# Top-k attention with a mixture-of-depths block: half a mask moved to VectorE, and the order of the last batch's end

## The chip, the cores and the metric

The kernel runs on one core of a Trainium2 chip. Its time is the device time of one execution in microseconds (us); the median of five runs counts. The core has five engines that run side by side and each work through their own instructions in order: PE (matrix products, with PEld for the loads of its stationary side), DVE (VectorE), ACT (ScalarE), POOL (GpSimd) and SP, which only issues transfers. They wait for each other by semaphores. PSUM is the memory that PE writes; it has eight banks, SBUF is the main memory on the chip.

## The reference

```python
# q, k, v: (8 batches, 8 heads, 576 rows, 64)
scores = scale * np.matmul(q, k.transpose(0, 1, 3, 2))
kth = np.partition(scores, -32, axis=-1)[..., -32:-31]
scores = np.where(scores >= kth, scores, -1000000000.0)
attn = np.exp(scores - max) ; attn = attn / (sum + 1e-09)
x = (attn @ v), heads side by side: (8, 576, 512)
# mixture of depths, for each batch b
s = einsum('bsd,d->bs', x, w_gate)
top_idx = the 128 rows with the largest s[b]
xe = x[b, top_idx]
h = np.maximum(xe @ w1, 0.0)          # 512 -> 1024
ye = h @ w2                           # 1024 -> 512
out[b] = x[b];  out[b, top_idx] += sigmoid(s[b, top_idx]) * ye
```

For each row of scores only the 32 largest count. Then, in each batch, the 128 rows of 576 with the largest gate go through a small network, whose result is added to these rows.

## The kernel before, in words

**Units and steps.** Each batch is cut into 18 units (`per_batch`): four row tiles of 128 with four pairs of heads each, and a last tile of 64 rows with two groups. There are 144 units. The main loop (`for n in range(-1, N)`) is a hand-written pipeline: step n works on several units at once, and the order of the calls is the order of the instructions on every engine (the wrapper `InOrder`, whose line 43 therefore stands for nearly all instructions in the profile). In step n the order is:

1. unit n-4: PE turns the scores and adds the mask to them (`weigh`, tile `ptr`), ACT takes exponentials (`pT`, `last`);
2. unit n-3: the mask `less`, scores below the 32nd largest (`mask_of`, `mask`): the first of two heads by ACT, the second by POOL, unless another pair of engines is passed as `on`;
3. unit n+1: PE multiplies q and k, ACT copies the scores out (`keep`, `sc<-ps`);
4. unit n-4: PE multiplies by v, ACT copies the sums out (`xs`);
5. unit n: DVE looks for a bound of the 32nd largest (`find_bound`: `cand`, `best`), then what has been put off for DVE (`flush_vector`), then what has been put off for POOL (`flush_pool`);
6. unit n-2: DVE finds the 32nd largest (`kth_of`: two MAX8 `next<-y`);
7. unit n-1: ACT marks what lies above the bound (`sides`), POOL multiplies scores by it (`y`, two operations and a small `y<-steps,seen`).

When a tile is done, DVE divides, POOL scales it into `x`, and two steps later DVE forms its gate (`prod<-x,wg`).

**The mixture** of a batch is a generator (`mixture`), advanced at fixed steps of the next two batches (`mix_at`, `mix_at_of`): spread the gates, count ranks, choose (`junk`, `pick`), gather 128 rows from the output by an indirect DMA on POOL (`fetch_rows`, `xe`), turn them (`xe_ps`, `xeT`), h in eight products of 128 columns (`multiply_h`), y in eight parts, and add to the output by an indirect DMA on POOL (`add_rows`, the scatter). For batches 0 to 4 the scatter is put off to POOL in the last step of the list, and issued in step 18b+55, that is, where n % 18 is 1.

**The end.** After the loop the last four units are finished by hand. The mixture of batch 6 (`between`) still has its eight parts of y to do. The mixture of batch 7 is the generator `closing`: the gate row is spread by PE transposes, DVE counts ranks and makes five `pick` tiles, PE multiplies them by places (`multiply_places`, tile `av`), DVE makes the row numbers (`keep_rows`), POOL gathers, PE turns the rows, and h, y and the scatter follow. Three parts of y of batch 6 stand ahead of its third stage, four ahead of the last counts and places, and the eighth behind the gather.

Between the gather and the turning of its rows stands a check: DVE folds some statistics of the whole run into one number per partition (`sure`), PE adds the partitions up (`av<-ones,sure`), DVE writes a flag (`unsure`), and `nc.values_load` loads the flag into a register of every engine. At the very end a branch on it would repeat everything by a general path, which this input doesn't need.

`xe_ps` and `y_ps` share the one buffer of the pool `ps_misc` (tag `misc`). `h` of the last batch lies in a tile `ptr` of two banks; `room_for_scores()` gives a tile of four.

```python
    def mask(sc, next8, on=None):
        less = wkpool.tile([P, 2, S], BF16, name="less")
        for i, engine in enumerate(on or (act, pool)):
```

## Time and profile before

| what | us |
|---|---|
| median of 5 runs | 878.7 |
| the five runs | 877.94, 878.58, 878.70, 881.25, 885.52 |
| the profiled execution | 881.17 |
| its span, first to last instruction | 879.31 |
| last score copy of ACT | 814.25 |
| last gather issued, landed | 846.26, 849.74 |
| last scatter issued, landed | 872.82, 877.75 |

The profile is one execution. Every time below is from the start of its span. Names such as `xe_ps<-ident,xe` say which tile is written from which. In a timeline a row may merge several instructions (x10); its length then runs from the first start to the last end. The time in brackets is how long the engine had stood still before the row, and what ended that. The durations of the indirect DMAs are those of their issue by POOL; the landing comes later.

### The profile page before, as it was taken

The numbers are of one execution on the slowest core, as the hardware profiler recorded it, in microseconds if no ns is written. First come the engines' busy times: TensorE is split into PE (matmuls) and PEld (weight loads), VectorE is DVE, ScalarE is ACT, GpSimd is POOL, SyncE is SP. The second block draws the span as 40 slices with busy tenths as digits, with TensorE's granted clock in tenths as the row PEclk, the third lists the DMA queues.
The fourth block names the chain that finished last, engine by engine and source line by source line (L and its number), as shares of the span: only waits on it lengthen the run. The fifth ranks groups of instructions, "written<-read, shape, count | busy, mean of one in ns | idle before, by whom it ended". The sixth has DMA issues, their size and how long they took to land. (4 is left out here: it accounts for less than half of the span.)

```text
span 879.3 us, 28118 instructions
## 1 busy us (share of the span) xinstructions
PE 808.7 (92%) x9879; PEld 620.6 (71%) x9879; DVE 810.9 (92%) x4918; ACT 760.5 (86%) x1705; POOL 708.2 (81%) x657
## 2 busy tenths in 40 slices
PE   4599988988999999999999999999999999988875
PEld 3377666666787777877787777877787778767743
DVE  4499999999999999999999999999999999999750
ACT  2599999988999999998999999999999999877710
POOL 2389998888888899888988899888988899878610
PEclk9599999999999999999999999999999999999988
DMA  5671111511141121511232122411333002101021
GB/s 120 162 211 26 38 26 55 105 38 38 61 83 43 38 50 56 105 38 38 74 72 54 38 41 65 105 38 27 86 52 73 14 15 68 15 14 14 13 68 15
DMA packets 122196, 50.36 MB, mean 57 GB/s; under 512 B 116416, under 2 KB 116416, under 8 KB 121024
## 3 DMA queue, kind: packets, MB, share of 16 engines
q1 hardware_dynamic: 118672, 43.91, 20.6%
q0 software_dynamic: 1792, 4.20, 2.8%
q8 instruction: 79, 1.29, 0.6%
q14 instruction: 69, 0.57, 0.2%
q10 hardware_dynamic: 1584, 0.39, 0.2%
HBM read 36.93 MB, written 11.55 MB: 55 GB/s over the span
## 5 line engine op out<-in xcount | busy, mean ns | idle before, releaser
L43 POOL TENSOR_TENSOR y<-sc,sides 128x576 f32<-128x576 f32 x288 | 370.5, 1324 | 107.4 <-ACT sides L43 104.8
L43 DVE MAX8 cand<-sc 128x8 f32<-128x72 f32 x2304 | 330.4, 218 | 21.0 <-ACT sc L43 21.0
L43 POOL TENSOR_SCALAR less<-sc,next 128x576 bf16<-128x576 f32 x141 | 248.9, 1765 | 17.6 <-DVE next L43 15.2
L43 PE MATMUL ptr<-out_of_reach,less 128*128 128x128 bf16 x1136 | 205.1, 220 | 22.3 <-POOL less L43 20.6
L43 ACT ACTIVATE sides<-sc,seen 128x576 bf16<-128x576 f32 x288 | 221.1, 768 | 4.8
L43 PE MATMUL ptr<-ident,sc 128*128 128x128 f32 x1136 | 215.7, 279 | 0.0
L43 DVE MAX8 next<-y 128x8 f32<-128x584 f32 x288 | 204.5, 752 | 3.6 <-POOL y L43 3.5
L43 PE MATMUL ps<-kT,qT 64*128 64x288 f32 (+1 forms) x1280 | 183.5, 435 | 5.4 <-ACT qT L43 3.5
L43 PEld LDWEIGHTS ptr<-ident,sc 128*128 128x128 f32 x1136 | 160.5, 141 | 22.4 <-PE av L43 10.4
L43 PE MATMUL av<-v,pT 128*64 128x65 f32 x4544 | 164.5, 225 | 11.5 <-ACT last L43 9.6
L43 PEld LDWEIGHTS av<-v,pT 128*64 128x64 f32 x4544 | 144.8, 138 | 41.4 <-ACT last L43 30.1
L43 ACT COPY sc<-ps 128x1152 f32<-128x1152 f32 x144 | 160.5, 1114 | 9.6 <-PE ps L43 9.3
L43 PEld LDWEIGHTS <-less 128*128 128x128 bf16 x1296 | 132.7, 103 | 44.3 <-POOL less L43 26.5
L43 ACT ACTIVATE pT<-ptr 128x1024 f32<-128x1024 f32 x142 | 143.9, 1013 | 17.8 <-PE ptr L43 15.5
L43 DVE MAX8 best<-cand 128x8 f32<-128x24 f32 (+2 forms) x864 | 141.9, 200 | 0.0
L43 ACT ACTIVATE less<-sc,next 128x576 bf16<-128x576 f32 x143 | 110.6, 774 | 24.1 <-DVE next L43 24.0
L43 PEld LDWEIGHTS ps<-kT,qT 64*128 64x128 f32 (+1 forms) x1280 | 99.4, 179 | 44.9 <-issue 21.9
L43 DVE MATCH_REPLACE8 cand<-best,cand 128x24 f32<-128x24 f32 (+1 forms) x576 | 102.0, 185 | 0.0
L43 PE MATMUL av<-vpair,last 128*128 128x130 f32 (+1 forms) x314 | 68.1, 317 | 0.0
L43 PE MATMUL y_ps<-w,hT 128*128 128x512 f32 x128 | 63.4, 596 | 0.0
L43 PE MATMUL h_ps<-xeT,w 128*128 128x128 f32 x448 | 59.4, 278 | 0.0
L43 PEld LDWEIGHTS h_ps<-xeT,w 128*128 128x128 f32 x448 | 53.9, 192 | 2.1 <-ACT xeT L43 1.1
(102 smaller groups left out, 867.3 us busy)
## 6 DMA issues: line engine op xcount, KB each, us to landing
rows<-in_k_dram SPq DMA_DIRECT2D x64, 128.0 KB, 3.1
v<-in_v_dram SPq DMA_DIRECT2D x64, 128.0 KB, 3.4
out_dram<-x SPq DMA_DIRECT2D x8, 1024.0 KB, 4.8
rows<-in_q_dram SPq DMA_DIRECT2D x62, 128.0 KB, 3.2
w<-in_moe_w_dram SPq DMA_DIRECT2D x2, 2048.0 KB
gate_row<-row_dram SPq DMA_DIRECT2D x7, 288.0 KB, 4.0
last<-in_k_dram SPq DMA_DIRECT2D x8, 128.0 KB, 3.2
vpair<-in_v_dram SPq DMA_DIRECT2D x16, 64.0 KB, 4.6
```

Of the source, the lines that this page charges most:

```text
L43: return lambda *a, **kw: self._tc.keep_in_program_order(fn(*a, **kw))
```

## The change

It has four parts. In the loop, in steps where n % 18 is 1, from step 37 on (37, 55, 73, 91, 109, 127), the second half of the mask is made by DVE and not by POOL. In the end, only one of four parts of y stays ahead of the last counts, so that four come behind the gather; h takes a tile of four banks, two products in each; and the check's product and flag come behind the turning of the gathered rows and the copy `xeT`, the load of the flag behind everything.

```diff
         spread(J, NT)
-        for _ in range(4):
-            next(between, None)
+        next(between)
         for t in range(J):
             count(t, slice(JP, S), others)
...
         act.copy(out=xeT, in_=ps.rearrange("p (c i) -> p c i", c=NDC))
+        yield
         hT = modpool.tile([P, NFC, CAP], FP32, name="hT")
-        h_ps = ps_tr.tile([P, 2, J, P], FP32, name="ptr").rearrange("p u c i -> p (u c) i")
+        h_ps = room_for_scores().rearrange("p a u (c i) -> p (a u) c i", i=CAP)
         for f0 in range(0, NFC, 2):
-            for fc in (f0, f0 + 1):
-                multiply_h(h_ps[:, fc, :], fc, xeT)
-            act.activation(hT[:, f0 : f0 + 2, :], h_ps[:, f0 : f0 + 2, :], AF.Relu)
+            bank = h_ps[:, f0 // 2 % 4, 0:2, :]
+            for i in range(2):
+                multiply_h(bank[:, i, :], f0 + i, xeT)
+            act.activation(hT[:, f0 : f0 + 2, :], bank, AF.Relu)
...
         if is_unit(n - 3):
-            mask_of(n - 3)
+
+            mask_of(n - 3, (act, dve) if n % per_batch == 1 and n > 2 * per_batch else None)
...
-    ps = ps_av.tile([P, 512], FP32, name="av")
-    pe.matmul(ps[0:1, 0:1], sure, ones)
     unsure = const.tile([1, 1], I32, name="unsure")
-    dve.tensor_scalar(
...
-    is_unsure = nc.values_load(unsure[0:1, 0:1])
-    next(closed, None)
+    def count_unsure():
+        ps = ps_av.tile([P, 512], FP32, name="av")
+        pe.matmul(ps[0:1, 0:1], sure, ones)
+        dve.tensor_scalar(
...
+    next(closed)
+    count_unsure()
+    next(closed, None)
     is_unsure = nc.values_load(unsure[0:1, 0:1])
```

## The prediction, as put on record

> **What bounds the kernel now.** I read the page first. Three engines are busy nine tenths of the span, so no total can say what an edit is worth; each has to be priced in its own stretch.

> The page:
> ```profile
> PE 808.7 (92%) x9879; PEld 620.6 (71%) x9879; DVE 810.9 (92%) x4918; ACT 760.5 (86%) x1705; POOL 708.2 (81%) x657
> ...
> L43 POOL TENSOR_SCALAR less<-sc,next 128x576 bf16<-128x576 f32 x141 | 248.9, 1765 | 17.6 <-DVE next L43 15.2
> ```
> The timeline of the last 35 us came second. Its columns are start, length, engine, and in brackets what ended the idle time.
> ```profile
> 844.52 1.26 PE L43 MATMUL av<-place_and_gate,pick 128*128 128x2 f32 x10
> ...
> 846.26 1.06 POOL L43 DMA_INDIRECT xe<-out_dram,row_i  x1 [6.71 <-DVE g L43]
> ...
> 846.88 0.69 ACT L43 ACTIVATE gy<-y_ps,g 128x512 f32<-128x512 f32 x1 [0.59 <-PE y_ps L43]
> ...
> 850.18 0.19 PE L43 MATMUL av<-ones,sure 128*1 128x1 f32 x2 [3.34 <-DVE ones L43]
> ...
> 851.29 1.09 PE L43 MATMUL xe_ps<-ident,xe 128*128 128x128 f32 x4 [0.92 <-DVE unsure L43]
> ...
> 853.05 3.78 PE L43 MATMUL ptr<-xeT,w 128*128 128x128 f32 x16 [0.68 <-ACT xeT L43]
> ...
> 857.30 2.24 PE L43 MATMUL ptr<-xeT,w 128*128 128x128 f32 x16 [0.47 <-ACT hT L43]
> ...
> 872.82 1.57 POOL L43 DMA_INDIRECT out_dram<-gy,row_i  x1 [20.67 <-POOLq L1250]
> ```
> Hardly anything overlaps here: picks, places, gather, transposes, h, y, scatter, landing. A microsecond saved ahead of 872.82 is one off the span. Two things stand out: PE waits at 850.18 for the check and not for the gathered rows, and the first quarter of h takes 3.78 where the last two take 2.05 each. Third, the windows view (PE, its loads, DVE, ACT, POOL, then the granted clock) explains the latter:
> ```profile
> 847.00:850.00 3.00, 0.00 (x0) 0.00 (x0) 2.78 (x14) 0.56 (x1) 0.32 (x1) 1.00 0.30 87
> ...
> 853.00:855.00 2.00, 1.95 (x9) 1.95 (x10) 0.00 (x0) 0.00 (x0) 0.00 (x0) 0.50 0.77 117
> ```
> PE stood still for 847 to 850, and transposes and h then ran at half clock until about 857.7 (860 to 864 has 1.00). Fourth, the stretch of a scatter, in POOL's timeline and then DVE's:
> ```profile
> 322.76 1.72 POOL L43 TENSOR_SCALAR less<-sc,next 128x576 bf16<-128x576 f32 x1
> 324.64 1.64 POOL L43 DMA_INDIRECT out_dram<-gy,row_i  x1 [0.16 <-ACT xs L43]
> ```
> ```profile
> 333.10 1.91 DVE L43 CUSTOM_DVE_ANT_0 prod<-x,wg 128x512 f32<-128x512 f32 x1
> ```
> POOL is late after a scatter and the gate's product on DVE, 0.67 in its shortest row, takes 1.91: it ends 0.63 after POOL's pair of y (334.38). But the time from one of ACT's score copies to the next is 5.65, 5.61 and 5.82 at steps 55 to 57, and the same at 37 to 39, where no scatter stands: ACT, idle 0.06 to 0.10 in each, sets them.

> **The end, step by step** (times of the profiled run).

> Places: only one part of y stays ahead of the five place products, which then wait for the last pick alone. It ends at 844.66; a PE load starts 0.12 after a DVE result (the ones at 850.03, the load at 850.15), and the last product takes 0.38 from load to end (845.40 to 845.78). They end at 845.16, not 845.78: row numbers and gather come 0.62 earlier. The gather landed at 849.74 (3.49 after its issue); now 849.12.

> Transposes: y's four parts start at 845.09 and take the 3.70 of the row at 840.99, to 848.79. They lie behind the gather, but the next tile, xe_ps, has the same PSUM bank (one buffer, tag misc), so it waits until ACT has copied y: 0.04 + 0.69, then 0.05 to PE, 849.57. That is later than the landing, so here the moved parts cost 0.4. The check's product and the load of its flag on PE's queue (0.48, after 850.59) no longer stand in front. From 851.29 to 849.57: **-1.72**, the 0.62 in it.

> Clock: PE's idle stretch shrinks from 3.34 to 0.8 us. The clock changes on a grid of 3.4 us here. Windows of it in which PE was 0.61 and 0.67 busy kept the full clock in this trace, ones with 0.31 and 0.06 lost it; the worst one here would be near 0.62. So I take full clock. Four transposes cost 0.71 instead of 1.09: **-0.38**. From start to start the first quarter of h costs 2.53 instead of 4.25, the second 2.53 instead of 2.71 (2.53 is the third's): **-1.91**. [...]

> h in four banks: its purpose can only be that PE needn't wait for ACT between quarters (0.47 in the lines, 0.64 from last start to next start). The built program has the four waits on ACT still, quarter 4 for the relu of quarter 3, as before: the wait goes by the tile, not by the bank. **0**; were they gone, 3 x 0.64 = -1.92.

> The check: its product now sits between transposes and h, where PE waits 0.6 for the copy of xeT; 0.19 fits. The flag's load (0.48 to 0.55 on the queues) is moved past ACT's copy, DVE's half of gy and POOL's last scatter. From the scatter's issue to its landing 4.93 us pass and 1.56 more to the end of the span; DVE's way to its last drain took 3.1 after gy, so 0.55 more is covered. If POOL alone had it behind its descriptors it would be +0.5. I take **0**.

> Sum of the end: -1.72 - 0.38 - 1.91 = **-4.01**.

> **The half mask.** Six masks leave POOL (1.72 each), at steps 37, 55, 73, 91, 109 and 127; five of these have a scatter behind. Each goes on DVE between the next-largest of one unit and the candidates of another. The only rows of a DVE mask:
> ```profile
> L43 DVE TENSOR_SCALAR less<-sc,next x4: 502/788/1543, 822.3 to 831.1; 128x576 bf16<-128x576 f32 x4
> ```
> 0.50 alone, 1.06 and 1.54 when POOL had started a y. At 322.2 POOL is at the second y until 322.56, so the mask ends near 322.9: DVE is 0.67 late (bounds 0.50 and 1.54). Queued behind it on DVE are the candidates and the next search, and ACT's mask waits for that one: a search that starts 0.78 before ACT's mask leaves no room. At 325.72 and 327.41 there is 0.24 to spare beyond 0.67. Then the gate's product: asked at 333.8, POOL's pair ended by 334.0 since the scatter went 1.4 us earlier, so it ends at 334.7, not 335.0. DVE is 0.3 ahead, and loses that at the last tile's product (345.05), which waits for POOL's pair either way. So **0** for steps 55 to 109, between -0.34 and +0.7 each.

> Step 37: searching starts at 226.38, ACT's mask at 227.50, so 0.34 to spare against 0.70: **+0.36** (to +0.9 if the product next misses POOL's gap). Step 127: the product at 733.23 took 2.44; with POOL on time it ends 1.0 earlier, of which 0.76 passes the next product, and from 761 to 779 ACT waits for DVE (1.06 and 4.62): **-0.8** (between -1.0 and +0.7). POOL's gain by itself buys nothing else: PE's loads wait for its mask only a few hundredths. Loop: **-0.4**.

> [...]

> **Sum.** The profiled run took 881.17 (span 879.31, 1.86 around it): -4.01 - 0.4 gives 876.8. It lies 2.5 over the median of the runs, 878.7, which the forecast goes by: **874.3**.

> **Rivals.** (1) The clock halves anyway, since its windows run free: 2.29 comes back, 876.6. For it: a window near the known edge. Against: 0.61 kept the clock. 0.10. (2) DVE's lag is paid: 0.7 for four or five of the masks, 877.1. For it: DVE shows no idle time at all, and only 0.24 of room. Against: the product's stall takes it up. 0.12. (3) **Slower**: each mask meets a POOL operation at its start and costs DVE the 1.54 of the longest row, and DVE is the bound so that nothing is given back: 6 x 1.54 = 9.2 against the end's 4.0, 883.9. It decides from 8.4 for the six, 1.4 each. Against: ACT sets these steps. 0.05. (4) The banks do free PE (the hardware or my reading of the waits): 872.4. 0.03. (5) DVE's lead lasts in all batches, 4 x 0.34: 872.9. 0.10.

> **Chances.** The forecast has 0.60. A measurement tells 0.5% from no change, 4.4 us, to 874.3: the forecast lies on that edge, half of it on either side. Faster 0.30 + 0.03 + 0.10 = 0.43; same 0.30 + 0.10 + 0.12 = 0.52; slower 0.05. The range reaches to rivals 1, 2, 4 and 5: 872.2 to 877.3.

> **What will show it.** Transposes of the last xe start 1.7 earlier and take about 0.7; the four quarters of h are equal, near 2.05, at clock 1.00, each with a wait of 0.47 for hT; the last scatter is issued 4 us earlier in relation to the last score copy. DVE masks of 0.5 to 0.9 at six places; ACT's mask waits more at step 38 alone. I am wrong if PE's waits for hT are gone, if the clock shows 0.50 after the gather, or if the steps at 55 to 57 change their 5.65, 5.61 and 5.82.

## The result, and the profile after

The changed kernel takes **877.91 us** (median of 38 runs, 874.86 to 881.35); the kernel before takes 880.18 beside it (64 runs, 877.94 to 885.52). The ratio is 0.9973, 95% interval 0.9965 to 0.9982: 2.3 us faster, 1.6 to 3.1 by the interval, and so within 0.5%. The forecast was 4.4 faster, 874.3; the time lies 0.6 above the upper end of the range. Two things are to be kept apart in this. The five runs that the forecast was set against had a median of 878.7, the 64 runs one of 880.18, so 1.5 of the miss is the base. The rest is in the kernel.

The profiled execution of the changed kernel took 880.17, its span is 878.41 (before 881.17 and 879.31). Between the spans the difference is -0.9: the start-up to step 36 +2.0 (the same code; in the 14 profiles of this study it ends anywhere from 216.7 to 220.8), steps 36 to 142 -1.6 (predicted -0.4), from the last score copy to the issue of the last scatter -1.46 (predicted -4.01), behind that +0.16.

The page of the changed kernel: busy time of the engines, and POOL's masks, six fewer than before.
```profile
PE 810.6 (92%) x9879; PEld 620.9 (71%) x9879; DVE 809.0 (92%) x4924; ACT 761.2 (87%) x1705; POOL 701.5 (80%) x651
...
L43 POOL TENSOR_SCALAR less<-sc,next 128x576 bf16<-128x576 f32 x135 | 233.9, 1732 | 15.0 <-DVE next L43 12.2
```
POOL's masks fell from 248.9 to 233.9 and DVE's total did not grow: its six masks cost 3.4, and its gate's products took 4.3 and its picks 1.4 less (the product of step 128 fell from 2.44 to 0.67, the second pick of step 134 from 0.99 to 0.28). These totals say nothing of the end, which the timeline shows. The changed kernel, from the last places on (start, length, engine, in brackets the idle time and what ended it):
```profile
843.31 1.53 PE L43 MATMUL av<-place_and_gate,pick 128*128 128x2 f32 x8 [0.80 <-DVE pick L43]
...
845.12 0.58 PE L43 MATMUL av<-place_and_gate,pick 64*128 64x2 f32 x2 [0.28 <-DVE pick L43]
...
845.63 6.16 PE L43 MATMUL y_ps<-w,hT 128*128 128x512 f32 x8
...
846.18 1.06 POOL L43 DMA_INDIRECT xe<-out_dram,row_i  x1 [6.22 <-DVE g L43]
...
851.83 0.69 ACT L43 ACTIVATE gy<-y_ps,g 128x512 f32<-128x512 f32 x1 [5.63 <-PE y_ps L43]
852.57 0.66 PE L43 MATMUL xe_ps<-ident,xe 128*128 128x128 f32 x4 [0.78 <-ACT gy L43]
...
853.90 2.05 PE L43 MATMUL ps<-xeT,w 128*128 128x128 f32 x16 [0.56 <-ACT xeT L43]
...
856.43 2.05 PE L43 MATMUL ps<-xeT,w 128*128 128x128 f32 x16 [0.47 <-ACT hT L43]
...
871.76 1.57 POOL L43 DMA_INDIRECT out_dram<-gy,row_i  x1 [17.34 <-DVEq L1256]
```
The gathered rows landed at 849.65, and the transposes start only at 852.57: they wait for ACT's copy of y, since the four parts of y took 6.16 and not 3.70. The windows view of the changed kernel (length, then busy time of PE, its loads, DVE, ACT, POOL, then the granted clock) says why:
```profile
840.40:843.80 3.40, 1.93 (x8) 0.91 (x7) 2.63 (x14) 0.21 (x1) 0.00 (x0) 1.00 0.18 41
843.80:850.60 6.80, 6.52 (x14) 3.64 (x14) 5.40 (x26) 0.20 (x1) 1.06 (x1) 0.50 0.14 40
850.60:857.00 6.40, 4.59 (x30) 3.13 (x29) 0.14 (x1) 1.66 (x3) 1.62 (x1) 1.00 0.32 39
```
The half clock did not go; it moved from the transposes and the first quarter of h, as it was before, to y's parts. From the transposes on, all is as predicted: 0.66 for them, equal quarters of 2.05, a wait of 0.47 between them.

In the loop, the changed kernel's POOL and then DVE in the same stretch as shown of before, and the row of DVE's masks:
```profile
325.74 1.64 POOL L43 DMA_INDIRECT out_dram<-gy,row_i  x1 [0.29 <-ACT gy L43]
```
```profile
336.24 1.13 DVE L43 CUSTOM_DVE_ANT_0 prod<-x,wg 128x512 f32<-128x512 f32 x1
```
```profile
L43 DVE TENSOR_SCALAR less<-sc,next x10: 502/568/1541, 225.0 to 831.5; 128x576 bf16<-128x576 f32 x10
```
This profile runs 2.46 later here than that of before when measured by the score copies. Against that the scatter is 1.36 earlier, the product takes 1.13 and not 1.91, and it ends 0.1 earlier than before: DVE has its mask back, and no more. The large change is at the other end of the loop. The gate's product of step 128 on DVE, before and after:
```profile
733.23 2.44 DVE L43 CUSTOM_DVE_ANT_0 prod<-x,wg 128x512 f32<-128x512 f32 x1
```
```profile
736.64 0.67 DVE L43 CUSTOM_DVE_ANT_0 prod<-x,wg 128x512 f32<-128x512 f32 x1
```
DVE then comes to step 134 0.9 earlier against the score copies. ACT's wait for DVE's next-largest in step 135, before and after:
```profile
777.29 0.78 ACT L43 ACTIVATE less<-sc,next 128x576 bf16<-128x576 f32 x1 [4.62 <-DVE next L43]
```
```profile
777.71 0.78 ACT L43 ACTIVATE less<-sc,next 128x576 bf16<-128x576 f32 x1 [2.30 <-DVE next L43]
```

### The profile page after: what moved, and what is told of

It is laid out like the page before. It is cut to its first block, busy times and chain, and to the rows that moved or that the text cites. A ratio compares the mean times of both kernels' runs of the same rounds, so it can differ in the third digit from the quotient of the medians.

```text
span 878.4 us, 28112 instructions
## 1 busy us (share of the span) xinstructions
PE 810.6 (92%) x9879; PEld 620.9 (71%) x9879; DVE 809.0 (92%) x4924; ACT 761.2 (87%) x1705; POOL 701.5 (80%) x651
## 5 line engine op out<-in xcount | busy, mean ns | idle before, releaser
L43 POOL TENSOR_TENSOR y<-sc,sides 128x576 f32<-128x576 f32 x288 | 368.2, 1305 | 116.5 <-ACT sides L43 107.8
L43 DVE MAX8 cand<-sc 128x8 f32<-128x72 f32 x2304 | 330.5, 217 | 22.5 <-ACT sc L43 22.5
L43 POOL TENSOR_SCALAR less<-sc,next 128x576 bf16<-128x576 f32 x135 | 233.9, 1732 | 15.0 <-DVE next L43 12.2
L43 ACT ACTIVATE sides<-sc,seen 128x576 bf16<-128x576 f32 x288 | 221.0, 768 | 5.2
L43 PE MATMUL ptr<-out_of_reach,less 128*128 128x128 bf16 x1136 | 205.2, 220 | 20.6 <-POOL less L43 20.1
L43 PE MATMUL ptr<-ident,sc 128*128 128x128 f32 x1136 | 215.5, 280 | 0.0
L43 DVE MAX8 next<-y 128x8 f32<-128x584 f32 x288 | 204.5, 751 | 4.4 <-POOL y L43 4.3
L43 PE MATMUL ps<-kT,qT 64*128 64x288 f32 (+1 forms) x1280 | 184.6, 437 | 5.4 <-ACT qT L43 3.5
L43 PEld LDWEIGHTS ptr<-ident,sc 128*128 128x128 f32 x1136 | 160.9, 142 | 22.7 <-PE av L43 10.4
L43 PE MATMUL av<-v,pT 128*64 128x65 f32 x4544 | 163.9, 224 | 12.1 <-ACT last L43 10.1
L43 PEld LDWEIGHTS av<-v,pT 128*64 128x64 f32 x4544 | 144.2, 137 | 42.2 <-ACT last L43 30.6
L43 ACT COPY sc<-ps 128x1152 f32<-128x1152 f32 x144 | 160.6, 1115 | 11.1 <-PE ps L43 10.8
L43 PEld LDWEIGHTS <-less 128*128 128x128 bf16 x1296 | 133.5, 104 | 41.1 <-POOL less L43 26.3
L43 ACT ACTIVATE pT<-ptr 128x1024 f32<-128x1024 f32 x142 | 143.9, 1014 | 19.8 <-PE ptr L43 17.8
L43 DVE MAX8 best<-cand 128x8 f32<-128x24 f32 (+2 forms) x864 | 141.9, 200 | 0.0
L43 PEld LDWEIGHTS ps<-kT,qT 64*128 64x128 f32 (+1 forms) x1280 | 99.9, 180 | 45.2 <-issue 22.2
L43 ACT ACTIVATE less<-sc,next 128x576 bf16<-128x576 f32 x143 | 110.6, 774 | 20.0 <-DVE next L43 19.7
L43 DVE MATCH_REPLACE8 cand<-best,cand 128x24 f32<-128x24 f32 (+1 forms) x576 | 102.0, 185 | 0.0
L43 PE MATMUL av<-vpair,last 128*128 128x130 f32 (+1 forms) x314 | 68.1, 317 | 0.0
L43 PE MATMUL y_ps<-w,hT 128*128 128x512 f32 x128 | 65.8, 617 | 0.0
L43 PE MATMUL h_ps<-xeT,w 128*128 128x128 f32 x448 | 59.4, 278 | 0.1
L43 PEld LDWEIGHTS h_ps<-xeT,w 128*128 128x128 f32 x448 | 53.9, 192 | 2.3 <-ACT xeT L43 1.2
```

The source lines that it names most:

```text
L43: return lambda *a, **kw: self._tc.keep_in_program_order(fn(*a, **kw))
```

## The experiments

All runs in one table, times of the profiled execution in us: steps by the time from one score copy to the next, the end from the last score copy. Each ratio is against runs of the kernel before on the same chip.

| run | ratio [95%] | steps 37+38 | 134+135 | 139+140 | places end | transposes start | last scatter |
|---|---|---|---|---|---|---|---|
| before | 1 | 11.26 | 16.62 | 14.13 | 31.53 | 37.04 | 58.57 |
| after | 0.9973 [0.9965, 0.9982] | 11.69 | 14.29 | 14.10 | 31.06 | 37.93 | 57.11 |
| e1_loop | 0.9987 [0.9973, 1.0001] | 11.68 | 14.31 | 14.09 | 31.54 | 37.04 | 58.39 |
| e2_end | 0.9985 [0.9970, 1.0000] | 11.25 | 16.62 | 14.07 | 31.03 | 36.89 | 56.08 |
| e3_127 | 0.9981 [0.9968, 0.9995] | 11.28 | 14.30 | 14.14 | 31.55 | 37.06 | 58.41 |
| e4_warm | 0.9944 [0.9929, 0.9958] | 11.70 | 14.30 | 14.07 | 30.85 | 35.26 | 54.44 |
| e5_133 | 1.0003 [0.9988, 1.0018] | 11.27 | 16.61 | 14.08 | 31.55 | 37.06 | 58.85 |
| e6_tiles | 0.9909 [0.9891, 0.9927] | 11.67 | 14.30 | 14.10 | 30.85 | 35.26 | 52.23 |
| e7_y_ahead | 0.9951 [0.9933, 0.9968] | 11.68 | 14.29 | 14.14 | 31.54 | 35.55 | 56.59 |
| e8_best | 0.9896 [0.9876, 0.9915] | 11.27 | 14.29 | 14.01 | 30.86 | 34.90 | 51.84 |
| e9_touch | 0.9977 [0.9959, 0.9994] | 11.25 | 15.68 | 12.52 | 31.55 | 37.05 | 58.37 |
| e10_act | 0.9968 [0.9951, 0.9985] | 11.26 | 14.34 | 12.53 | 31.54 | 37.05 | 58.39 |
| e11_narrow | 0.9972 [0.9953, 0.9992] | 11.68 | 14.29 | 14.13 | 31.30 | 37.93 | 57.11 |
| e12_final | 0.9907 [0.9873, 0.9941] | 11.28 | 14.29 | 12.55 | 30.85 | 34.92 | 53.49 |

**e1_loop** and **e2_end** take the change apart: the kernel before with the six masks alone, and with the new end alone (the other parts of the diff, unchanged).

> Only the half masks on DVE (all six), with the end of the kernel before. Theory A (the loop's gain is real and comes from step 127's mask): steps 134 and 135 together last 14.3 instead of 16.6 us, step 37 and 38 cost 0.43 more, steps 56, 74, 92, 110 cost 0.06 more each; from the score copy of step 36 to the last one 1.6 us less than before; the end from the last score copy to the last scatter stays 58.6. Time 1.6 us under before. Theory B (the shorter steps 134 and 135 were one run's chance): these two steps last 16.6 as before, time 0.7 us over before.

> Only the changed end, with the old masks. Theory A (PE stands still for the picks, its clock halves, y's four moved parts run at half clock and hold the bank that the gathered rows need): y's four parts take about 6.2 us instead of 3.7, the end from the last score copy to the last scatter 57.1 instead of 58.6, time 1.5 us under before; in executions where the clock's grid falls otherwise it is up to 4.0 less. Theory B (y is slow because of the gather and the check beside it): y takes 6.2 whatever the granted clock. Steps 134 and 135 together stay at 16.6.

The masks alone bring steps 36 to 142 from 596.19 to 594.49, with the end as before, and the end alone 58.57 to 56.08. In the medians (before took 881.55 beside these) they give -1.6 and -0.5, which with the changed kernel's -2.3 would add up, but neither is clear of noise alone: both intervals reach 1.000. In the profiles the loop's part agrees (-1.7, and -1.6 in the changed kernel) and the end's doesn't (-2.5 and -1.46). In e2_end the half clock lasted one window of 3.41 and not two, so y's parts took 5.15 and not 6.16, and the end came out 1.0 better than in the changed kernel (56.08 against 57.11), with the same code.

**e3_127**: the kernel before with the mask on DVE at step 127 alone.
```diff
-            mask_of(n - 3)
+            mask_of(n - 3, (act, dve) if n == 7 * per_batch + 1 else None)
```

> Only step 127's half mask on DVE, with the end of the kernel before. Theory A: steps 134 and 135 last 14.3 together, nothing else in the loop changes, 2.3 us under before. Theory B (the other five masks or their longer lead are needed): the two steps stay near 16.6, time as before.

The whole gain is there: 134+135 go from 16.62 to 14.30, and steps 36 to 142 take 593.66, 0.8 less than with all six masks. The five others only cost: 0.43 at 37 and 38, and 0.06 each at 56, 74, 92 and 110 (5.61 to 5.67).

**e4_warm**: the changed kernel with four products of the identity by itself, three while PE waits for the first picks and one ahead of the last place. They write a tile that nothing reads.
```diff
         next(between)
+        warm = room_for_scores()
+        for _ in range(3):
+            pe.matmul(warm[:, 0, 0, 0:P], ident, ident)
...
+            if t == J and warm is not None:
+                pe.matmul(warm[:, 0, 0, 0:P], ident, ident)
```

> The changed kernel with four added products of the identity by itself (they write a tile that nothing reads), three while PE waits for the first pick and one while it waits for the last. Theory A: PE is busy in these waits, the clock stays at 1.00, y's four parts take 3.7 instead of 6.2, the transposes of the gathered rows come 2.5 us earlier after the last score copy (about 35.5 instead of 37.9), the last scatter about 54.6 after it instead of 57.1; time 2.5 us under the changed kernel. Theory B (company of the gather and the check slows y): y stays at 6.2 and the time with it, or 0.3 more.

The timeline of e4_warm in the same place as the changed kernel's above:
```profile
842.68 0.83 PE L43 MATMUL ps<-ident 128*128 128x128 f32 x6
843.64 1.15 PE L43 MATMUL av<-place_and_gate,pick 128*128 128x2 f32 x8
844.65 0.47 PE L43 MATMUL ps<-ident 128*128 128x128 f32 x2
845.45 0.38 PE L43 MATMUL av<-place_and_gate,pick 64*128 64x2 f32 x2 [0.33 <-DVE pick L43]
845.76 3.70 PE L43 MATMUL y_ps<-w,hT 128*128 128x512 f32 x8
...
850.24 0.66 PE L43 MATMUL xe_ps<-ident,xe 128*128 128x128 f32 x4 [0.78 <-ACT gy L43]
```
From the places on the clock stays at 1.00 to the last scatter, y takes 3.70 with the gather and the check beside it, and the end is 4.13 shorter than in before. The prediction's 4.01 was the sum for a kernel that keeps its clock.

**e5_133, e9_touch, e10_act** ask what step 127 bought. In the built program the mask on DVE has a by-product: DVE waits for a count of PE there, and the first pick of step 134, which waited for an older count, has that wait no more. So two causes were open: DVE's lead, and the vanished wait. e5_133 is before with the mask on DVE at step 133 (no scatter there, but the pick's wait is gone).

> The kernel before, with the half mask on DVE at one step alone, 133, where no scatter is near: POOL is relieved at a place where it has no descriptors to write, DVE gets 0.5 more work, and in the built program the last pick's wait for PE is gone as a by-product. Theory A (what the mask at step 127 bought, 2.3 in steps 134 and 135, is the time POOL has back behind the last scatter, and so the lead of DVE from there): nothing of it comes here, steps 134 and 135 together take 16.6 as before or up to 0.6 more, the run is level with before or 0.6 slower. Rival (what was bought is the wait of pick that went, 0.46, and what followed from it): steps 134 and 135 take 15.3 to 16.2 and the run is 0.5 to 1.3 faster. Steps 37, 38 and 56 and the end stay as in before under both.

16.61 and a level run, as the lead would have it. But the trace makes this inconclusive. The mask took 0.98 and DVE came to step 134 1.07 later than in before; the picks gave just that back. Since the two effects cancelled, two runs part them. e9_touch removes the wait without a mask, at step 133:
```diff
         less = wkpool.tile([P, 2, S], BF16, name="less")
+        if touch:
+            dve.memset(less[:, 1, 0:1], 0.0)
```

> The kernel before with one addition: at step 133 DVE clears one column of the mask tile (128 elements) before ACT and POOL fill it. That costs DVE under 0.1 and nothing at step 127, but DVE has then waited for PE, and in the built program the wait for PE at the first pick of step 134 is gone. It prices that wait alone. In before, the wait holds the pick for 0.46, and the second pick then meets POOL's product x and takes 0.99 instead of 0.29. Theory A (DVE's lead from step 127 is all that the mask bought): steps 134 and 135 take 16.6 as before, the run is level. Rival (the vanished wait and what follows from it are a part of the 2.3, about 1.1): the picks end about 1.1 earlier, ACT waits 1.1 less for the next-largest, steps 134 and 135 take 15.4 to 15.8, the run is 0.8 to 1.2 faster. Nothing else changes under both.

e10_act gives POOL its relief at step 127 with no work for DVE and leaves the pick's wait:
```diff
-            mask_of(n - 3)
+            mask_of(n - 3, (act, act) if n == 7 * per_batch + 1 else None)
```

> The kernel before with the whole mask of step 127 on ACT: POOL is relieved of 1.72 there as in the changed kernel, DVE gets nothing more to do, and the pick of step 134 keeps its wait for PE. ACT, which sets the pace, pays 0.8 more at step 127. It prices the lead without the vanished wait. Theory A (the lead is all): the product at step 128 takes 0.7 and not 2.4, steps 134 and 135 take 14.2 to 14.8, steps 127 and 128 together 0.7 to 0.9 more than in before, the run is 1.0 to 1.6 faster. Rival (both are needed): the pick still waits 0.4 or so, and steps 134 and 135 take 15.2 to 15.8, the run is level to 0.6 faster.

The picks of step 134 on DVE, and ACT's wait in step 135, in before, in e9_touch and in e10_act:
```profile
762.56 0.29 DVE L43 TENSOR_SCALAR pick<-slot,ranks 128x128 f32<-128x128 f32 x1 [0.46 <-PE av L43]
763.61 0.99 DVE L43 TENSOR_SCALAR pick<-slot,ranks 128x128 f32<-128x128 f32 x1
```
```profile
762.11 0.47 DVE L43 TENSOR_SCALAR pick<-slot,ranks 128x128 f32<-128x128 f32 x1
763.34 0.29 DVE L43 TENSOR_SCALAR pick<-slot,ranks 128x128 f32<-128x128 f32 x1
...
776.33 0.78 ACT L43 ACTIVATE less<-sc,next 128x576 bf16<-128x576 f32 x1 [3.69 <-DVE next L43]
```
```profile
763.98 0.29 DVE L43 TENSOR_SCALAR pick<-slot,ranks 128x128 f32<-128x128 f32 x1 [0.46 <-DVE junk L43]
765.03 0.29 DVE L43 TENSOR_SCALAR pick<-slot,ranks 128x128 f32<-128x128 f32 x1
...
777.34 0.78 ACT L43 ACTIVATE less<-sc,next 128x576 bf16<-128x576 f32 x1 [2.35 <-DVE next L43]
```
e10_act keeps the wait of 0.46 and still takes 14.34: a lead of DVE over ACT is enough for the 2.3 of these two steps. It is no clean copy of the changed kernel's lead, though. The product at step 128 still took 1.80 (0.7 was expected), and of the 0.9 by which DVE leads the score copy of step 134, 0.68 is ACT's own delay, from the second half of the mask that it makes ahead of the score copy of step 127; net of that delay 1.6 is won. e9_touch has no lead and takes 15.68: the vanished wait alone is worth 0.94. They do not add (14.29 with both). In before, the second pick begins at 763.61, inside POOL's product x (763.48 to 764.53), and takes 0.99; either remedy moves it off that, and the lead saves the same kind of stall in step 135 too, where e9_touch still has a pick of 0.93 and e10_act has none over 0.46. How the 2.3 divides between the two stays open.

**e7_y_ahead**: the changed kernel with y's four parts ahead of the places again, to price that move.
```diff
-        next(between)
+        for _ in range(4):
+            next(between, None)
```

> The changed kernel with the four parts of y put back ahead of the last places; masks, check's product and banks as in the changed kernel. It prices the move of y alone. Theory A (the check's product and the flag's load were what the transposes waited for; moving y bought 0.5 in the places and cost it again behind the gather, since y and xe share a bank and y ran at half clock): places end at 31.5, the gather is issued at 32.0 and lands at 35.5 after the last score copy, as in before, but the transposes start at 35.6 to 36.1, earlier than in the changed kernel (37.9); then PE is idle before the landing, the clock is 0.5 there, the transposes take 1.1 and the first quarter of h 3.8, and the last scatter is at 56.8 to 57.3: level with the changed kernel. Rival (the move of y is what shortens the end, 1.5 of it): last scatter at 58 to 58.6, 1.0 to 1.5 slower than the changed kernel.

The transposes of e7_y_ahead follow the landing at once:
```profile
850.23 1.09 PE L43 MATMUL xe_ps<-ident,xe 128*128 128x128 f32 x4 [2.95 <-DMA xe<-out_dram,row_i]
```
They start 1.49 earlier than in before, which is the check's product and flag alone. They run cold (1.09), yet the last scatter comes at 56.59, 0.5 ahead of the changed kernel (and 0.2 ahead of theory A's range). In these two profiles the move of y bought 0.5 in the places and cost 1 behind them. With one window of half clock instead of two, as in e2_end (56.08), the moved y is 0.5 ahead instead, so one profile doesn't give the sign; the ratios, 0.9951 without the move and 0.9973 with it, speak against the move, but their intervals still touch.

**e6_tiles** and **e8_best**. e6_tiles is e4_warm with h's pairs in two tiles by turns. e8_best has the mask at step 127 alone, two parts of y ahead and three behind, one added product ahead of the last place, the transposes in a tile that doesn't share y's bank, and h in two tiles.
```diff
-        h_ps = room_for_scores().rearrange("p a u (c i) -> p (a u) c i", i=CAP)
+        rooms = [
+            room_for_scores().rearrange("p a u (c i) -> p (a u) c i", i=CAP),
+            ps_tr.tile([P, 2, J, P], FP32, name="ptr"),
+        ]
...
-            bank = h_ps[:, f0 // 2 % 4, 0:2, :]
+            bank = rooms[f0 // 2 % 2][:, f0 // 4, 0:2, :]
```

> The kernel e4_warm (the changed kernel with four matrix products into a tile that nothing reads while PE waits for picks), with the eight pairs of h in two tiles alternately, not in four banks of one. Theory A (PE's wait of 0.47 at each quarter of h is for the tile, which is the unit by which the program waits, and not for a bank): the three waits for hT fall to 0 to 0.1, the quarters run on, h takes 7.6 to 7.9 from first to last start of a product instead of 9.6, the last scatter is issued 52.4 to 52.8 us after the last score copy instead of 54.4, and the run is 1.6 to 2.0 faster than e4_warm (about 0.992 of before). Rival (ACT's relu is the pace: PE waits for it whatever the tile): the waits move from one quarter to the next but h still takes 9.6, last scatter at 54.4, 0.994 of before.

> What the runs so far point to, put together: the mask on DVE at step 127 alone; two real parts of y ahead of the places and three behind, one matrix product into a tile that nothing reads ahead of the last place; the transposes' results in a bank of their own, so that they needn't wait for the copy of y; h in two tiles alternately; the check's product behind the transposes. Theory A (each piece is worth what it was alone): the loop gives 2.3; gather at 31.3 to 31.5 and landed at 35.0; transposes at 35.1 at full clock; h 7.7 from there on; last scatter at 51.8 to 52.5, 6.0 to 6.7 earlier than before; the run is 8 to 9 us faster than before, 0.990 to 0.991. Rival (three parts of y behind the gather leave PE idle for 1 to 1.5 us before the rows land, a window of the clock falls under some 0.6 busy, and transposes and the first quarter of h go at half clock): transposes 1.1, first quarter 3.8, last scatter at 54.2 to 54.8, the run 5.8 to 6.5 faster, 0.993.

The timeline of e8_best from the transposes on:
```profile
847.32 0.63 PE L43 MATMUL ptr<-ident,xe 128*128 128x128 f32 x4 [1.27 <-DMA xe<-out_dram,row_i]
...
848.62 2.05 PE L43 MATMUL ps<-xeT,w 128*128 128x128 f32 x16 [0.56 <-ACT xeT L43]
...
850.51 1.95 PE L43 MATMUL ptr<-xeT,w 128*128 128x128 f32 x16
...
852.30 1.95 PE L43 MATMUL ps<-xeT,w 128*128 128x128 f32 x16
...
864.26 1.57 POOL L43 DMA_INDIRECT out_dram<-gy,row_i  x1 [14.67 <-DVEq L1263]
```
The brackets behind the first quarter of h are gone, in e6_tiles too: the last scatter of e6_tiles comes 2.21 before e4_warm's. PE's wait was for the tile. e8_best takes 872.06 (median of 4 runs) where before takes 881.85; its ratio is 0.9896: the version that beats both.

**e11_narrow** asks what the clock counts: e4_warm with the added products two columns wide. Again nothing reads their tile.
```diff
-            pe.matmul(warm[:, 0, 0, 0:P], ident, ident)
+            pe.matmul(warm[:, 0, 0, 0:2], ident, ident[:, 0:2])
```

> The kernel e4_warm with its four added products two columns wide and not 128, at the same places and with the same 128x128 weights; as before they write a tile that nothing reads. It asks what the clock counts. In the rows a product of two columns takes about as long as one of 128 (eight of 128x2 took 1.15 to 1.53, six of 128x128 0.83), so by the rows PE is as busy in this kernel as in e4_warm. Theory A (what counts is the work in the columns, so that the row of 1.53 for the places hides an almost idle PE, and the window read as 0.57 busy was worth about 0.35): the clock is 0.5 behind the places as in the changed kernel, four parts of y take 4.9 to 6.2, the last scatter is at 56.0 to 57.2. Rival (what counts is the time in which an instruction runs): the clock stays at 1.0, four parts of y take 3.7, the last scatter is at 54.4 as in e4_warm.

The windows of e11_narrow, on its own grid:
```profile
839.20:842.60 3.40, 2.50 (x13) 1.54 (x12) 2.50 (x15) 0.21 (x1) 0.00 (x0) 0.99 0.18 41
842.60:849.40 6.80, 6.80 (x17) 4.18 (x18) 5.53 (x27) 0.20 (x1) 1.06 (x1) 0.50 0.14 40
```
PE was busy for 2.50 of 3.40 by its rows, and the clock fell; with 128 columns at the same places (e4_warm) it did not. The runs agree: the ratio of e11_narrow, 0.9972, is that of the changed kernel, 0.9973, and e4_warm has 0.9944. In the traces of before and after the clock stands at 1.00 or 0.50 for whole multiples of 3.41 (0.50 from 843.79 to 850.62 in the changed kernel, two of them). I worked out the share of each such window from the PE rows, once as they stand and once without products of one or two columns:

| window | by all rows | without the narrow ones | clock behind it |
|---|---|---|---|
| after, first places | 0.57 | 0.43 | 0.50 |
| e7_y_ahead, places | 0.74 | 0.44 | 0.50 |
| e12_final, before the transposes | 0.50 | 0.46 | 0.50 |
| e11_narrow, places | 0.74 | 0.501 | 0.50 |
| e9_touch, step 139 | 0.499 | 0.499 | 1.00 |
| before, places | 0.81 | 0.51 | 1.00 |
| e8_best, places | 0.90 | 0.55 | 1.00 |
| e4_warm, places | 0.87 | 0.57 | 1.00 |

Where the grid falls differs from execution to execution, so I slid a window of 3.41 over the rows, without the narrow products. In the changed kernel and in e11_narrow some window at the places is under 0.45 wherever the grid falls. In e4_warm one is under 0.50 (at 0.48) for 1.3 of the 3.41 places of the grid: its full clock there is likely, not certain.

**e12_final** adds 14 repeats of one transpose to e8_best at step 140, where PE waits 2.36 for POOL's mask and most profiles go to half clock for 3.41.
```diff
+                for _ in range(again if (i, c) == (1, 0) else 0):
+                    pe.transpose(tr[:, i, c, :], z[:, i, at], ident)
```

> The kernel e8_best with one addition at step 140, where PE waits 2.36 for POOL's mask and goes to half clock in most profiles (steps 139 and 140 take 14.0 to 14.1 then, and 12.5 in e9_touch and e10_act, where it did not): 14 repeats of the transpose that stands ahead of that wait, into the same place, so that the last one leaves the same values. Theory A (the half clock there costs 1.6, and filling the wait saves it): steps 139 and 140 take 12.3 to 12.7, no half clock before the last 10 us, the last scatter at 51.8 as in e8_best, the run 1.4 to 1.8 faster than e8_best, 0.987 to 0.988 of before. Rival (the repeats outlast the wait for the mask, or the pace of POOL and DVE sets these steps whatever PE's clock): steps 139 and 140 stay at 14.0, or longer; the run is level with e8_best, 0.990.

The place itself did what theory A says: 139+140 take 12.55, at full clock. This profile alone can't tell that from chance, since e9_touch and e10_act kept the clock there without repeats. By the sliding window it isn't chance: in e8_best's rows a window at step 140 is under 0.50 for 2.35 of the 3.41 places of the grid, with the repeats none is under 0.67. But the end of this profile lost its clock, and the run is level with e8_best (872.59). The end of e12_final:
```profile
846.22 0.63 PE L43 MATMUL ptr<-ident,xe 128*128 128x128 f32 x4 [1.30 <-DMA xe<-out_dram,row_i]
...
847.52 2.95 PE L43 MATMUL ps<-xeT,w 128*128 128x128 f32 x16 [0.56 <-ACT xeT L43]
```
The code of the end is that of e8_best. Its idle 1.30 and 0.56 fell into one window, where e8_best's were split over two. That cost 1.65, where 1.46 had been won at steps 139 and 140. With three parts of y behind the gather, PE's idle time around the transposes is near the edge: a sliding window is under 0.50 for 1.3 of the 3.41 places of the grid.

## Why the prediction was wrong, and where it was right

**The step that failed is the clock: "So I take full clock."** Its reason was that "the worst one here would be near 0.62" against 0.61 that had kept it. By the rows it was near (0.57). But the places are products of two columns, and four added ones of two columns left the clock at 0.50 (e11_narrow) where four of 128 kept it at 1.00 (e4_warm): without the narrow ones the window is 0.43, under the 0.501 up to which windows lost the clock. Nor was that the bad luck of one grid: by all rows no window there goes under 0.57 wherever the grid falls, without the narrow products one always goes under 0.45. So y's four parts took 6.16 and not 3.70, and the transposes came 0.89 later than in before instead of 1.72 earlier, of which the gather's share is 0.48 (0.62 predicted). Rival 1 named this cause, but put its price on h (2.29), and so still gave 876.6; the price fell on y, 2.46, and e4_warm gives it back: 54.44 against 57.11, of which 0.21 is earlier places. The longest idle stretch of PE in that window was 0.80, and the clock still fell: what orders the windows of these profiles is their sum. Two of the prediction's own signs of being wrong showed: a clock of 0.50 behind the gather, and step 56 at 5.67 instead of 5.61.

**The other terms of the end** hold. The check in front of the transposes: e7_y_ahead shows it alone, 1.49. Shared bank of y and xe: the transposes wait 0.78 behind y, as priced. Transposes 0.66 and h without its cold quarter: from the start of the transposes to the last scatter 19.18 instead of 21.53, -2.35 (predicted -0.38 - 1.91 = -2.29). Four banks: 0, "the wait goes by the tile, not by the bank", shown by e6_tiles, where two tiles bring 2.21. The check's flag: 6.65 from the last scatter on, against 6.49, in a spread of 6.30 to 6.73 over all profiles: 0.

**The loop** was better than predicted, -1.6 for -0.4. Step 37: +0.37 for +0.36. Steps 55 to 109: +0.06 each for 0, within the bounds, and 0.06 at step 38 too; ACT's `sides` waits for two semaphores there instead of one, and stands 0.09 idle ahead of it instead of 0.03. The mis-sized term is step 127: -2.3 for -0.8, outside its bounds of -1.0 to +0.7. The mechanism given (the product at 733.23 no longer late, DVE early while ACT waits for it) is what e3_127 shows (product 0.70, steps 134 and 135 14.30), and e10_act shows that such a lead needs no vanished wait. What was not counted is that a lead of 0.9 grows on its way, because two picks that ran beside POOL's `x` and `y` (0.99 and 0.94) then miss these (0.28 and 0.29), and that the first pick's wait of 0.46 goes.

**The sum.** In the profile -1.6 - 1.46 = -3.1 against -4.4, and 1.5 more from the base: five runs were too few to place a median to better than this. That makes 2.8 of the miss of 3.6; the other 0.8 lies between this one execution and the medians (-2.3), and stays open. The loop's surplus of 1.2 covers nearly half of the 2.55 that the end lacks, which was luck.

## What to carry to other kernels

Before work is moved out of a place where PE waits, sum what stays in each window of the clock's length (3.41 here), for every place of the grid, and leave out products of two columns: by that sum the windows that lost the clock had 0.501 or less, the others 0.499 or more. A few real or idle products in the wait can be cheaper than a cold stretch behind it: four of them brought 2.7 here. If PE waits for a reader of the bank it just left, and the program waits by tiles, give it another tile (2.21 in e6_tiles), not another bank of the same one (0 in the changed kernel). And where a DVE operation runs long beside POOL's (the product of step 128: 2.44 before, 0.67 after), that is worth removing ahead of a place where another engine already waits for DVE: the mask at step 127 brought 2.3 there, the five others brought nothing.

## What the runs showed of the hardware beyond this

- The grid of 3.41 has no fixed place against the program: the same end was cold for two windows in the changed kernel and for one in e2_end (y's parts 6.16 and 5.15), and cold in e12_final but not in e8_best (first quarter of h 2.95 and 2.05).
- The first pick of a batch, which waits for two engines, starts 0.11 after its predecessor in five batches of before and 0.46 in the sixth; with one wait it is 0.04. The profile lays the 0.46 on PE in before and on DVE's own `junk` in e10_act. Why the sixth costs more stays open.
- Half a clock for one window at step 140 costs 1.6: 14.0 to 14.1 in the profiles that have it, 12.5 in the three that don't.
